# A retention and two mixture-of-experts layers on one core: decays taken relative to one fixed position, and the work of the attention put in order by tables

## The chip, the cores and the metric

One program runs on one core of a Trainium2 chip. The metric is the time of an execution on the device in microseconds (us). Five engines work side by side, each in its own fixed order: TensorE (PE in the profile; PEld is its loading of weights), VectorE (DVE), ScalarE (ACT), GpSimd (POOL) and SyncE (SP), which issues all the DMAs. An engine whose next instruction waits for a semaphore holds everything behind it.

## The reference, cut to what matters

Shapes: batch 2, 8 heads, 768 positions, head size 64. So there are 1536 tokens of width 512.

```
gamma = 1.0 - 2.0 ** (-5.0 - arange(H))
for t in range(S):                                   # the attention
    state = gamma * state + k[t] (outer) v[t]
    y[t]  = (1 / sqrt(D)) * q[t] @ state
x = y.reshape(B * S, H * D)
logits = x @ w_gate; P = exp(logits - max)           # first mixture, 8 experts
for _ in range(8): P /= P.sum(1); P /= P.sum(0); P *= N / E
out = sum over e of P[:, e] * (relu(x @ w1[e]) @ w2[e])
# second mixture, 4 experts: the same with p = domain_probs / its row sum
```

## The kernel before, in words

The attention is done in 12 chunks of 128 positions, 6 of each batch (chunk i, with c its place in the batch). For each chunk q, k (as head size by position) and kn, v (position by head size) are loaded, 256 KB each; the last chunk of a batch needs no kn. Heads go in pairs, so a [128, 512] tile holds all 8.

- Scores (`att_scores`, L242): 8 matmuls k by q into two PSUM banks. DVE multiplies both by a mask that holds the decay (L246), which gives `a`.
- `att_prep` on POOL: `ks` is kn scaled by a decay (L225), `qs` is q scaled by a decay and by the 1/sqrt(D) (L231).
- State (`att_decay`, `att_state`): POOL decays the state held in SBUF into `sg` (L253), PE makes the chunk's own part (L263), and DVE adds both into the other one of two tiles S (L276, two instructions; a copy at L271 for a batch's first chunk).
- Output (`att_out`): PE adds qs by S (L288) and v by a (L293) in one of two PSUM banks called chain. The chunks c = 0 to 2 go through `first_half`, the others through `second_half`. These make the inputs of the first layer's matrix products: every input is kept as a high part (fp32r, made by ACT) and a low part (the rest), and four differences (T1 to T4) are needed, since the products are done by a 7-product scheme. ACT copies the bank to SBUF (L144, L155), DVE makes the differences (L152) and the low parts (L78).

The attention is written out by hand as a loop over the chunks: load and prepare chunk i+2, scores of i+1, state of i, the leftover pieces of chunk i-1, output of i. Chunk buffers: three for q, k and v, two for kn. Into the same loop go the loads and splits of the first expert's weights (w1: four raw blocks of 256 KB; sums at L117, high parts on ACT at L124, low parts on POOL at L128) and the gate's logits (L347: 8 matmuls for the first half of a batch, 12 for the second).

Then come 48 units: each does one half of one expert for one batch, 168 matmuls of 128x384 (L494). Their order is set by tables: each piece has a place, and all pieces are sorted by it (`UNIT_AT`, `W_AT`). The first unit needs only batch 0's inputs and the first weights; its first product M1 is the first row of L494. Pieces of the last chunk are left for it.

Of the kernel before, what the change touches and what calls it, by code (L numbers as in the profile page):

```python
# [14 lines left out]
C_MASK, C_QT, C_ID, C_ONE, C_G, C_K, C_SEL, C_END = 0, 1024, 1536, 1664, 1792, 1796, 1804, 1812  # L15
# [8 lines left out]
def retention_moe_moe(ctx: ExitStack, tc: tile.TileContext, qT, kT, kN, vN, cst, wg, dprob, w1a, w2a, w1b, w2b, out):  # L24
# [114 lines left out]
    def first_half(key, b, j, pa, xa):  # L139


        hi, lo = (t[:, :, j * P:(j + 1) * P] for t in xt[key, b]["A"])
        n = 4 if key == 1 else 2
        return [lambda: nc.scalar.activation(out=xa[:, 0:n], in_=pa[:, 0:n], func=AF.Copy), lambda: split(hi, lo, pa)]  # L144

    def second_half(key, b, j, pb, xa, xb, b21):


        x = {k: [t[:, :, j * P:(j + 1) * P] for t in v] for k, v in xt[key, b].items()}

        def sub(to, a, b_):
            nc.vector.tensor_tensor(out=to, in0=a, in1=b_, op=ALU.subtract)  # L152

        def b12():
            nc.scalar.activation(out=xb[:, 0:2], in_=pb[:, 0:2], func=AF.Copy)  # L155

        def sums13():
            sub(xa[:, 0:2], pb[:, 0:2], xa[:, 0:2])
            sub(xb[:, 0:2], pb[:, 2:4], xb[:, 0:2])

        def sums24():
            sub(xb[:, 2:4], pb[:, 2:4], xa[:, 0:2])
            sub(xa[:, 2:4], b21, xb[:, 2:4])

        return [b12, lambda: split(*x["B22"], pb[:, 2:4]), sums13, sums24,
                lambda: split(*x["TA"], xa), lambda: split(*x["TB"], xb)]

    def x_block(key, b, k):
        kk, o = {"B11": ("A", 0), "B21": ("A", 2), "B22": ("B22", 0), "T1": ("TA", 0), "T2": ("TB", 2),
                 "T3": ("TB", 0), "T4": ("TA", 2)}[k]  # L170
        return [t[:, o:o + 2] for t in xt[key, b][kk]]

    with tc.manual_schedule():
# [40 lines left out]
        qtab = ap1.tile([P, NPR, CK], F32, name="qtab")
        nc.sync.dma_start(out=qtab, in_=cst[:, C_QT:C_ID].rearrange("p (h t) -> p h t", h=NPR))
        load_att(2, ("q", "k"))
        load_att(1, ("kn", "v"))
        nc.sync.dma_start(out=small[:, 0:C_G - C_ID], in_=cst[:, C_ID:C_G])

        def att_prep(i):  # L220
            b, c = chunks[i]
            t = att_in[i]
            if c < NCK - 1:
                ks = ap2.tile([P, H, D // H], F32, tag="ks", name="ks")
                nc.gpsimd.tensor_tensor(  # L225
                    out=ks, in0=t["kn"].rearrange("p (h d) -> p h d", h=H),
                    in1=ktab.unsqueeze(2).to_broadcast([P, H, D // H]), op=ALU.mult)
                t["ks"] = ks
            if c > 0:
                qs = ap2.tile([P, NPR, CK], F32, tag="qs", name="qs")  # L230
                nc.gpsimd.tensor_tensor(out=qs, in0=t["q"], in1=qtab, op=ALU.mult)  # L231
                t["qs"] = qs

        def att_scores(i):
            t = att_in[i]

            a = t["a"] = ap2.tile([P, 2, NPR, CK], F32, tag="a", name="a")
            p_ = [ps(), ps()]
            for pr in range(NPR):
                for z in range(2):  # L240
                    o = slice(64 * z, 64 * z + 64)
                    nc.tensor.matmul(  # L242
                        p_[z][:, pr * CK:(pr + 1) * CK], t["k"][o, pr, :], t["q"][o, pr, :],
                        start=True, stop=True, skip_group_check=True)
            for z in range(2):
                nc.vector.tensor_tensor(  # L246
                    out=a[:, z], in0=quads(p_[z]), in1=quads(mask[:, z]), op=ALU.mult)

        def att_decay(i):
            c = chunks[i][1]  # L250
            if 0 < c < NCK - 1:
                sg = att_in[i]["sg"] = ap1.tile([P, NPR, P], F32, tag="sg", name="sg")
                nc.gpsimd.tensor_tensor(out=sg, in0=S[c % 2], in1=gtab.unsqueeze(2).to_broadcast([P, NPR, P]), op=ALU.mult)  # L253

        def att_state(i):
            b, c = chunks[i]
            t = att_in[i]
            if c == NCK - 1:
                return
            p_ = ps()  # L260
            for h in range(H):
                o = slice(64 * (h % 2), 64 * (h % 2) + 64)
                nc.tensor.matmul(  # L263
                    p_[o, h * 64:(h + 1) * 64], t["ks"][:, h, :], t["v"][:, h * 64:(h + 1) * 64],
                    start=True, stop=True, skip_group_check=True)
            pv = p_.rearrange("p (r e) -> p r e", r=NPR)
            new = S[(c + 1) % 2]
            if c == 0:
                for z in range(2):
                    o = slice(64 * z, 64 * z + 64)  # L270
                    nc.vector.tensor_copy(new[o, :, o], pv[o, :, o])  # L271
            else:
                sg = t["sg"]
                for z in range(2):
                    o = slice(64 * z, 64 * z + 64)
# [667 lines left out]
```

## Time and profile before

| what | value |
|---|---|
| median of 3 runs | 1506.4 us (1506.12 to 1507.52) |
| profiled execution, span from first to last instruction | 1502.8 us |
| PE busy | 1474.6 us, 98% of the span |
| DVE, POOL, ACT busy | 73%, 69%, 49% |
| granted TensorE clock, mean | 0.993 of full speed |

The profile gives the span of its execution, which is 3.6 us under the median of the runs; what lies around the span is in that difference. A share of 98% for PE is an average over two stages: the attention at the start, in the first two of the 40 slices of the page, and the units. A busy PE counts matmuls as they lie in its pipeline, so where blocks are short, busy does not mean at its peak.

### The profile page before, as it was taken

To read this page: it belongs to the slowest core of one execution; us is meant where nothing else is said; L and a number is where in the kernel's file an instruction comes from. 1 tells how busy PE (TensorE), PEld (TensorE's weight loads), DVE (VectorE), ACT (ScalarE), POOL (GpSimd) and SP (SyncE) were. 2 spreads that over 40 slices of the span, in tenths; PEclk is the share of its full clock that TensorE was granted. 3 is DMA by queue.
4 is the path that set the end of the run, shared out by engine and by line. 5 is a ranking of instruction groups with operands and counts; after the bars stand their busy time and mean duration, and the time that the engine had idled before them with its cause. 6 is when DMAs were issued, how large, how long until landed. Compare 5 with 4: busy or idle time off the path is not lost.

```text
span 1502.8 us, 24372 instructions
## 1 busy us (share of the span) xinstructions
PE 1474.6 (98%) x8778; PEld 1457.2 (97%) x8778; DVE 1097.7 (73%) x2079; ACT 742.2 (49%) x1589; POOL 1038.6 (69%) x901
## 2 busy tenths in 40 slices
PE   8899999999999999999999999999999999999998
PEld 6799999999999999999999999998999999999998
DVE  5868877677777767776776776788667767777776
ACT  2355454455455444545544544555655445545552
POOL 5756587686676766856865866769958668677682
PEclk9999999999999999999999999999999999999999
DMA  9310112211211211121122112111121121121112
GB/s 294 113 29 29 30 50 61 67 39 40 78 39 39 58 59 39 39 78 40 39 57 61 39 39 78 40 39 39 57 60 39 40 77 39 39 73 45 39 47 88
DMA packets 97432, 86.23 MB, mean 57 GB/s; under 512 B 9376, under 2 KB 85280, under 8 KB 97312
## 3 DMA queue, kind: packets, MB, share of 16 engines
q1 hardware_dynamic: 97312, 84.69, 18.5%
q8 instruction: 68, 1.11, 0.3%
q14 instruction: 52, 0.43, 0.1%
HBM read 81.45 MB, written 3.22 MB: 56 GB/s over the span
## 4 chain that ended last, share of the span: by engine, by line
PE 88%; POOL 4%; DVE 4%; issue 2%; DMA 1%; SPq 0%; ACT 0%; DVEq 0%; POOLq 0%
PE ps L494 49%; PE chain L494 37%; POOL w L128 1%; POOL raw L117 1%; POOL h L554 1%; DMA kn<-in_kN 1%; DVE acc L481 1%; PE ps L347 1%; DVE xl L78 0%; DVE ps L481 0%; DMA raw<-in_w2a 0%; POOL acc L543 0%; POOL ev L617 0%; DMA k<-in_kT 0%; DVE acc L152 0%
## 5 line engine op out<-in xcount | busy, mean ns | idle before, releaser
L494 PE MATMUL ps<-h,w 128*128 128x384 f32 x2304 | 432.3, 335 | 1.8 <-POOL h L554 1.6
L494 PE MATMUL ps<-xh,w 128*128 128x384 f32 x1536 | 431.4, 336 | 0.6 <-ACT ev L478 0.5
L494 PEld LDWEIGHTS ps<-h,w 128*128 128x128 f32 x2304 | 402.2, 188 | 4.1 <-POOL h L554 3.1
L128 POOL TENSOR_TENSOR w<-raw,w 128x512 fp32r<-128x512 f32 x266 | 356.8, 1345 | 55.9 <-ACT w L124 55.8
L494 PE MATMUL chain<-xh,w 128*128 128x384 f32 x1152 | 332.9, 336 | 3.2 <-ACT ev L478 2.3
L494 PE MATMUL chain<-h,w 128*128 128x384 f32 x1728 | 333.2, 335 | 2.5 <-DVE acc L481 1.8
L554 POOL TENSOR_TENSOR h<-ev,h 128x384 fp32r<-128x384 f32 x288 | 292.9, 1032 | 45.0 <-ACT h L478 43.8
L617 POOL TENSOR_TENSOR ev<-ev,fac 128x384 f32<-128x384 f32 x96 | 98.3, 1024 | 301.9 <-DVE ps L613 301.2
L494 PEld LDWEIGHTS chain<-h,w 128*128 128x128 f32 x1728 | 302.5, 188 | 3.9 <-DVE acc L481 1.8
L494 PEld LDWEIGHTS ps<-xh,w 128*128 128x128 f32 x1536 | 282.8, 189 | 1.2 <-ACT ev L478 1.2
L124 ACT ACTIVATE w<-raw 128x512 fp32r<-128x512 f32 x336 | 205.1, 624 | 151.7 <-POOL raw L117 130.0
L117 POOL TENSOR_TENSOR raw<-raw 128x512 f32<-128x512 f32 x188 | 244.5, 1301 | 20.0 <-POOL w L128 13.7
L494 PE MATMUL ps<-xl,w 128*128 128x384 f32 x768 | 257.9, 336 | 0.0
L481 DVE TENSOR_TENSOR acc<-chain,acc 128x384 f32<-128x384 f32 x272 | 150.5, 554 | 105.3 <-PE chain L494 104.2
L554 DVE TENSOR_TENSOR h<-ps,h 128x384 fp32r<-128x384 f32 x384 | 210.8, 550 | 11.8 <-ACT h L478 3.3
L478 ACT ACTIVATE h<-ps 128x384 fp32r<-128x384 f32 x384 | 186.4, 488 | 65.5 <-DVE ps L481 61.8
L494 PEld LDWEIGHTS chain<-xh,w 128*128 128x128 f32 x1152 | 211.9, 188 | 4.8 <-ACT ev L478 3.1
L494 PE MATMUL chain<-xl,w 128*128 128x384 f32 x576 | 193.1, 335 | 1.8 <-POOL xl L758 1.8
L478 ACT ACTIVATE chain<-ps 128x384 f32<-128x384 f32 x192 | 92.0, 479 | 204.2 <-DVE acc L481 171.1
L481 DVE TENSOR_TENSOR acc<-ps,acc 128x384 f32<-128x384 f32 x272 | 145.3, 548 | 45.9 <-PE ps L494 45.9
L478 ACT ACTIVATE h<-ev 128x384 fp32r<-128x384 f32 x288 | 149.6, 520 | 45.1 <-DVE ev L557 40.9
L494 PEld LDWEIGHTS ps<-xl,w 128*128 128x128 f32 x768 | 145.3, 189 | 0.0
(116 smaller groups left out, 1181.6 us busy)
## 6 DMA issues: line engine op xcount, KB each, us to landing
fac<-rows SPq DMA_DIRECT2D x46, 384.0 KB
raw<-in_w1a SPq DMA_DIRECT2D x128, 128.0 KB
raw<-in_w2a SPq DMA_DIRECT2D x64, 256.0 KB
raw<-in_w1b SPq DMA_DIRECT2D x64, 128.0 KB
raw<-in_w2b SPq DMA_DIRECT2D x32, 256.0 KB
q<-in_qT SPq DMA_DIRECT2D x12, 256.0 KB
k<-in_kT SPq DMA_DIRECT2D x12, 256.0 KB
v<-in_vN SPq DMA_DIRECT2D x12, 256.0 KB
```

The lines of the kernel that those rows point to most:

```text
L117: eng.tensor_tensor(out=raws[s, k], in0=raws[s, a], in1=raws[s, b], op=op)
L124: nc.scalar.activation(out=t[0], in_=raws[s, k], func=AF.Copy)
L128: eng.tensor_tensor(out=lo, in0=raws[s, k], in1=f32(hi), op=ALU.subtract)
L347: nc.tensor.matmul(p_[:, 0:TH], l, r, start=(n == 0), stop=(n == len(mm) - 1))
L478: copy, relu = (lambda o, i, f=f: nc.scalar.activation(out=o, in_=i, func=f) for f in (AF.Copy, AF.Relu))
L481: nc.vector.tensor_tensor(out=out, in0=in0, in1=in1, op=op)
L494: nc.tensor.matmul(p_, l, r, start=(first and n == 0), stop=(n == len(mm) - 1), skip_group_check=True)
L554: eng.tensor_tensor(out=lo, in0=src, in1=f32(hi), op=ALU.subtract)
L617: nc.gpsimd.tensor_tensor(out=a22, in0=a22, in1=self.g_[:, 1], op=ALU.mult)
```

## The change

The decay of a key is now taken relative to one fixed position of the batch (the start of chunk `MID` = 2). v is scaled once per chunk by gamma to a power that depends on its position (`vs`, POOL), and this vs serves both the state and the product with a. The mask is then only 0 or 1, one [128, 128] tile. The state needs no decay between chunks: PE sums it over all chunks of a batch in one PSUM bank, which stays taken (`state`), and ACT copies it to S. q is used as it is. The output of a chunk is multiplied by a table (`scale`, DVE); the tables of chunks 1 to 5 are made by ACT, four instructions each, out of the one before (`dt`).

The differences are made in another form: the output no longer is copied by ACT; in chunks c = 0 to 2 scale writes it to SBUF, in the others it stays in its bank, and T2 and T3 go to a third bank (`self.q`). Low parts of A and TA go to POOL save for four pieces named in `ON_VECTOR`; three of the four weight sums go there as well. The second half's logits take 8 matmuls, with weights that hold the needed sums. At the start PE clears 9 times a bank with zeros in place of two fp32 matmuls; two matmuls before the units (L842) go.

Buffers for q, k, v and kn are four each. The constants shrink (the mask from 512 KB to 64 KB). The order of all pieces of the attention comes from tables by chunk (`CHUNK_AT`, one number for each batch) and for the other pieces (`MISC_AT`); the first unit and the first weights have tables of their own (`UNIT0_AT`, `W0_AT`).

```diff
+    def low(t, src, eng):
+        eng.tensor_tensor(out=t[1], in0=src, in1=f32(t[0]), op=ALU.subtract)
+
+    def high(t, src):
+        nc.scalar.activation(out=t[0], in_=src, func=AF.Copy)
+
+    def sub(to, a, b_):
+        nc.vector.tensor_tensor(out=to, in0=a, in1=b_, op=ALU.subtract)
...
+                t[nm] = ap2.tile([P, NPR, CK] if nm in "qk" else [P, D], F32, tag=nm, name=nm, bufs=4)
...
+        def clear(bank):
+            nc.tensor.matmul(bank, zero[:, 0:P], zero, start=True, stop=True, skip_group_check=True)
...
+        state = ps()
+        for c_ in 4 * chain + [state]:
+            clear(c_)
+
+        mask = ap1.tile([P, CK], F32, name="mask")
+        nc.sync.dma_start(out=mask, in_=cst[:, C_MASK:C_V])
+        tabs = ap1.tile([P, C_DT - C_V], F32, name="tabs")
+        nc.sync.dma_start(out=tabs, in_=cst[:, C_V:C_DT])
+        vtab = tabs[:, 0:C_G - C_V].rearrange("p (c h) -> p c h", h=H)
...
+            def vs(self):
+                t = self.t
+                t["vs"] = ap2.tile([P, H, D // H], F32, tag="vs", name="vs")
                 nc.gpsimd.tensor_tensor(
+                    out=t["vs"], in0=t["v"].rearrange("p (h d) -> p h d", h=H),
+                    in1=vtab[:, self.c].unsqueeze(2).to_broadcast([P, H, D // H]), op=ALU.mult)
+
+            def dt(self):
+                c = self.c
+                if self.b == 0 and c > 0:
+                    dtab[c] = ap1.tile([P, NPR, CK], F32, name=f"dtab{c}")
+                    for r in range(NPR):
+                        nc.scalar.activation(out=dtab[c][:, r], in_=dtab[c - 1][:, r], func=AF.Copy, scale=gtab[:, r:r + 1])
...
+                nc.vector.tensor_tensor(
+                    out=t["a"][:, z], in0=quads(t["p"][z]), in1=mask.unsqueeze(1).to_broadcast([P, NPR, CK]), op=ALU.mult)
...
-            new = S[(c + 1) % 2]
-            if c == 0:
-                for z in range(2):
-                    o = slice(64 * z, 64 * z + 64)
-                    nc.vector.tensor_copy(new[o, :, o], pv[o, :, o])
-            else:
-                sg = t["sg"]
-                for z in range(2):
-                    o = slice(64 * z, 64 * z + 64)
-                    nc.vector.tensor_tensor(out=new[o, :, o], in0=pv[o, :, o], in1=sg[o, :, o], op=ALU.add)
...
+                        state[o, h * 64:(h + 1) * 64], t["kn"][:, h * 64:(h + 1) * 64], t["vs"][:, h, :],
+                        start=False, stop=True, skip_group_check=True)
+
+            def S(self):
+                if self.c < NCK - 1:
+                    nc.scalar.activation(out=S[(self.c + 1) % 2], in_=quads(state), func=AF.Copy)
...
+                            self.o[:, pr], S[c % 2][:, pr, :], t["q"][:, pr, :], start=(pr == 0), stop=False, skip_group_check=True)
...
+            def scale(self):
+                xs[self.i] = quads(spare(self.i % 5))
+                to = self.o if self.half else xs[self.i]
+                nc.vector.tensor_tensor(out=to, in0=self.o, in1=dtab[self.c], op=ALU.mult)
+
+            def hA(self):
+                high(self.x("A"), xs[self.i])
+
+            def lA(self):
+                low(self.x("A"), xs[self.i], lower(f"lA{self.i}"))
+
+            def t12(self):
+                self.xa, self.xt = xs[self.i - TPH], xs[self.i]
+                self.q = self.o if self.last else quads(ps())
+                sub(self.xt[:, 0:2], self.o[:, 0:2], self.xa[:, 0:2])
+                sub(self.q[:, 0:2], self.o[:, 2:4], self.xt[:, 0:2])
+
+            def t4(self):
+                sub(self.xt[:, 2:4], self.xa[:, 2:4], self.q[:, 0:2])
+
+            def t3(self):
+                sub(self.q[:, 2:4], self.q[:, 0:2], self.xa[:, 0:2])
...
+            def lTA(self):
+                low(self.x("TA"), self.xt, lower(f"lTA{self.i}"))
+
+            def hTB(self):
+                high(self.x("TB"), self.q)
+
+            def lTB(self):
+                low(self.x("TB"), self.q, nc.vector)
...
-            parts = [("B11", 0), ("B21", 2)] if half == 0 else [("B11", 0), ("T1", 0), ("B22", 2)]
-            mm = [(wgs[:, o + c, :], x[:, c, :]) for k, o in parts for c in range(2) for x in x_block(1, b, k)]
+            parts = [("B11", 0), ("B21", 2)] if half == 0 else [("B22", 4), ("T3", 6)]
...
+        CHUNK_AT = {'load': (-5.779, -1.553), 'vs': (-1.56, -1.499), 'dt': (-2.533, -3.312), 'scores': (-0.823, -0.993), 'state': (0.146, 0.42), 'S': (0.148, 0.44), 'm0': (-0.505, -0.474), 'm1': (-0.113, -0.254), 'scale': (0.925, 0.587), 'hA': (1.552, 0.777), 'lA': (1.716, 2.293), 't12': (1.096, 0.873), 'hB': (1.104, 1.418), 't4': (1.241, 1.22), 't3': (1.37, 0.999), 'lB': (1.579, 1.813), 'hTB': (1.765, 1.569), 'hTA': (1.354, 1.651), 'lTB': (2.108, 1.884), 'lTA': (1.935, 1.869), 'inter': (0.866, 0.251), 'av': (0.867, 0.252)}
+        ON_VECTOR = ('+S2', 'lA0', 'lA6', 'lTA11')
...
+        for _, _, f, a in sorted(todo, key=lambda e: e[:2]):
+            f(a)
...
-        for c_ in (chain[1], chain[0]):
-            x_ = xt[1, 0]["A"][0].rearrange("p c t -> p (c t)")[:, 0:512]
-            nc.tensor.matmul(c_, w1t[0, "A11"][0][:, 0, 0, :], x_, start=True, stop=True, skip_group_check=True)
...
+            for name, places in {**UNIT_AT, **(UNIT0_AT if k == 0 else {})}.items():
```

On SP the four blocks of w1 are now loaded in three places: A11 ahead of chunk 3, A22 ahead of chunk 6 (with the gate's small inputs behind it), A21 and A12 between chunks 6 and 7. Before, all four stood behind chunk 5's v. Nothing else stands ahead of chunk 11's loads.

The order on two engines. PE from the scores of chunk 11 on, before (q, k are a chunk's inputs, a its masked scores, S the state's tiles, acc the gate's weights in L347):

```order
L242 MATMUL ps<-q,k 128x128 x8
L263 MATMUL ps<-v,ks 64x64 x8
L288 MATMUL chain<-qs,S_86 128x128 x4
L293 MATMUL chain<-a,v 64x128 x8
L288 MATMUL ps<-qs,S_87 128x128 x4
L293 MATMUL ps<-a,v 64x128 x8
L842 MATMUL chain<-xh,w_547 128x512 x2
L347 MATMUL ps<-xh,acc 128x384
```

The same from chunk 11's scores on, after:

```order
L260 MATMUL ps<-q,k 128x128 x8
L299 MATMUL chain<-q,S_86 128x128 x4
L306 MATMUL chain<-a,vs 64x128 x8
L285 MATMUL ps<-vs,kn 64x64 x8
L395 MATMUL ps<-xh,acc 128x384
L395 MATMUL ps<-xl,acc 128x384
```

Here 16 rows of L395, the logits of batch 0, now stand between the state of chunk 10 and the last two rows of the attention, L299 and L306 of chunk 11. After these come the 8 logits of batch 1's first half and M1, as before. In the kernel before, batch 0's logits stood ahead of chunk 10's and of chunk 11's scores.

DVE in the stretch from chunk 7's to chunk 8's scores, before (xl are low parts, raw the weight sums, S the state):

```order
L246 TENSOR_TENSOR a<-ps,mask 128x512 x2
L276 TENSOR_TENSOR S_86<-ps,sg 64x4x64 x2
L78 TENSOR_TENSOR xl<-chain,xh 128x4x128
L78 TENSOR_TENSOR xl<-acc,xh 128x4x128 x2
L117 TENSOR_TENSOR raw<-raw 128x512
L246 TENSOR_TENSOR a<-ps,mask 128x512 x2
```

And after, from chunk 7's masks on (dtab is the table of `scale`):

```order
L268 TENSOR_TENSOR a<-ps,mask 128x512
L313 TENSOR_TENSOR acc<-chain,dtab_119 128x512
L268 TENSOR_TENSOR a<-ps,mask 128x512
L141 TENSOR_TENSOR xl<-ps,xh 128x4x128
L268 TENSOR_TENSOR a<-ps,mask 128x512
L313 TENSOR_TENSOR acc<-chain,dtab_184 128x512
```

The state's two rows are gone, scale has come in between the two masks of a chunk, and the low parts that stand there read a PSUM bank.

## Rows read from the trace of the kernel before

**Rows 1.** Windows: span, busy us and count of each engine, clock, DMA share, GB/s.

```profile
0.00:10.00 10.00, 6.77 (x38) 4.04 (x40) 1.95 (x4) 1.28 (x1) 2.23 (x7) 1.00 0.81 279
10.00:20.00 10.00, 8.96 (x123) 7.92 (x124) 4.70 (x9) 2.17 (x4) 7.66 (x7) 0.83 0.94 286
20.00:30.00 10.00, 9.47 (x135) 8.11 (x134) 7.59 (x17) 2.06 (x6) 7.17 (x9) 1.00 0.96 288
30.00:40.00 10.00, 7.70 (x120) 6.69 (x120) 9.63 (x27) 3.70 (x9) 3.85 (x4) 1.00 0.98 331
40.00:50.00 10.00, 3.86 (x56) 3.34 (x56) 9.89 (x13) 3.16 (x6) 10.00 (x8) 0.89 0.62 207
50.00:60.00 10.00, 9.90 (x90) 8.64 (x91) 8.99 (x12) 3.04 (x6) 8.35 (x7) 0.77 0.08 30
...
300.00:1503.00 1203.00, 1194.58 (x6861) 1190.85 (x6859) 876.25 (x1626) 608.15 (x1305) 843.61 (x728) 1.00 0.17 51
```

**Rows 2.** Timeline (start, us, then the instructions), PE at the end of the attention.

```profile
68.91 0.34 PE L347 MATMUL ps<-xh,acc 128*128 128x384 f32 x1
...
70.32 0.33 PE L494 MATMUL ps<-xh,w 128*128 128x384 f32 x1
```

**Rows 3.** Waits of PE before 70.3 us: total, times, longest.

```profile
PE chain L288 <- DVE xl L78: 6.9, 3, 5.7
PE ps L242 <- DMA k<-in_kT: 2.4, 2, 1.9
```

**Rows 4.** Waits of SP's DMA queue before 75 us: total, times, longest.

```profile
SPq L190 <- PE chain L293: 14.5, 5, 8.2
```

**Rows 5.** Timeline, PE, first scores of batch 1.

```profile
31.57 1.16 PE L242 MATMUL ps<-q,k 64*128 64x128 f32 x16 [1.94 <-DMA k<-in_kT]
```

**Rows 6.** Timeline, PE, one chunk of batch 0 in order.

```profile
22.82 0.69 PE L263 MATMUL ps<-v,ks 128*64 128x64 f32 x16
...
23.44 1.15 PE L288 MATMUL chain<-qs,S 128*128 128x128 f32 x8
...
24.52 1.09 PE L293 MATMUL chain<-a,v 128*64 128x128 f32 x16
...
25.55 1.16 PE L242 MATMUL ps<-q,k 64*128 64x128 f32 x16
```

**Rows 7.** Timeline, PE after its longest wait.

```profile
50.10 2.05 PE L288 MATMUL chain<-qs,S 128*128 128x128 f32 x8 [5.67 <-DVE xl L78]
```

**Rows 8.** Groups by line and shape, DVE, before 70.3 us: busy, mean ns, idle before.

```profile
L246 DVE TENSOR_TENSOR a<-ps,mask 128x512 f32<-128x512 f32 x24 | 15.3, 681 | 12.5 <-PE ps L242 12.4
L78 DVE TENSOR_TENSOR xl<-acc,xh 128x512 fp32r<-128x512 f32 x8 | 10.1, 1296 | 0.0
L276 DVE TENSOR_TENSOR S<-ps,sg 64x256 f32<-64x256 f32 x16 | 6.7, 419 | 5.8 <-POOL sg L253 5.7
...
L117 DVE TENSOR_TENSOR raw<-raw 128x512 f32<-128x512 f32 x4 | 5.1, 1286 | 0.0
L78 DVE TENSOR_TENSOR xl<-chain,xh 128x512 fp32r<-128x512 f32 x6 | 4.2, 692 | 0.2
```

**Rows 9.** Groups by line and shape, POOL, before 70.3 us.

```profile
L231 POOL TENSOR_TENSOR qs<-q,qtab 128x512 f32<-128x512 f32 x10 | 13.8, 1384 | 0.0
L225 POOL TENSOR_TENSOR ks<-kn,small 128x512 f32<-128x512 f32 x10 | 11.5, 1154 | 18.6 <-DMA kn<-in_kN 18.6
L128 POOL TENSOR_TENSOR w<-raw,w 128x512 fp32r<-128x512 f32 x7 | 10.1, 1454 | 6.2 <-ACT w L124 6.2
L253 POOL TENSOR_TENSOR sg<-S,small 128x512 f32<-128x512 f32 x8 | 9.2, 1152 | 0.0
```

**Rows 10.** Groups by line and shape, ACT, before 70.3 us.

```profile
L144 ACT ACTIVATE acc<-chain 128x512 f32<-128x512 f32 x6 | 3.6, 593 | 27.3 <-PE chain L293 21.7 <-DVE xl L78 5.5
...
L155 ACT ACTIVATE acc<-chain 128x256 f32<-128x256 f32 x5 | 1.9, 379 | 12.0 <-PE chain L293 7.9 <-PE ps L242 4.1
```

**Rows 11.** Timeline, DVE, lows read from SBUF, POOL idle and POOL busy.

```profile
35.73 1.29 DVE L78 TENSOR_TENSOR xl<-acc,xh 128x512 fp32r<-128x512 f32 x2
...
40.94 3.43 DVE L78 TENSOR_TENSOR xl<-acc,xh 128x512 fp32r<-128x512 f32 x2
```

More of the change, by code (lines that the diff above doesn't have):

```diff
@@ L214, in retention_moe_moe @@
[L214 to L224, printed above, removed]
-                nc.gpsimd.tensor_tensor(
[L226 to L232, printed above, removed]
@@ new lines, in retention_moe_moe @@
+        ON_VECTOR = ('+S2', 'lA0', 'lA6', 'lTA11')
+        FIRST_AT = {'scores': -3.475, 'm1': -0.632, 'm0': -1.999, 'vs': -2.199, 'state': -0.219, 'scale': 1.183}
+        LAST_AT = {'t12': -2.17, 'hB': 1.35, 't4': -2.164, 'lB': 3.021, 't3': 3.1, 'hTB': 3.2, 'hTA': -0.104, 'lTB': 3.3, 'lTA': 0.876}
+        MISC_AT = {'loadA21': 4.489, 'loadA11': -3.686, 'loadA22': 2.159, 'loadA12': 5.383, 'small': 2.226, 'wgb': 7.217, 'wgs': 7.56, 'dp': 8.875, 'rows': 9.541, 'w2': 11.969, 'logits0': 10.877, 'logits1': 11.07, 'A11': 4.834, '+S3': 5.416, 'A22': 3.433, '+S1': 6.405, '+S2': 7.911, 'A12': 8.552, '+S4': 11.449, 'S1': 8.942, 'S2': 9.009, 'S3': 9.846, 'S4': 11.978}
@@ new lines, in misc @@
+        def misc(k):
+            if k.startswith("load"):
+                load_w1(0, (k[4:],))
+            elif k[0] == "+":
+                sum_of(0, k[1:], lower(k))
+            elif k[0] in "AS":
+                split_hi(0, k)
+                split_lo(0, k, lower(k))
+            else:
+                {"small": get_small, "wgb": sum_wg, "wgs": prep_wg, "dp": prep_dp, "rows": lambda: keep_rows(2, small_in["dpt"]),
+                 "w2": lambda: load_w2(0), "logits0": lambda: logits(0, 0), "logits1": lambda: logits(0, 1)}[k]()
@@ new lines, in retention_moe_moe @@
+        todo = [(p, n, misc, k) for n, (k, p) in enumerate(MISC_AT.items())]
+        final = []
+        for i in range(len(chunks)):
+            ch = Chunk(i)
+            for name, places in CHUNK_AT.items():
+                pos = places[ch.b]
+                if name in (LIGHT if ch.half else HEAVY) or (name == "load" and i < 3):
+                    continue
+                f = getattr(ch, name)
+                if ch.last and name in LAST_AT:
+                    final.append((LAST_AT[name], f))
+                    continue
+                if i == 0:
+                    pos = FIRST_AT.get(name, pos)
+                todo.append((i + pos, len(todo), lambda g: g(), f))
@@ L853, in retention_moe_moe @@
         for k, un in enumerate(units):
-            for name, places in UNIT_AT.items():
+            for name, places in {**UNIT_AT, **(UNIT0_AT if k == 0 else {})}.items():
                 for i, pos in enumerate(places):
@@ L873, in retention_moe_moe @@
                         at(k * L + pos, to_x2, un.b, name, c)
-        for pos, f in zip((-1, -0.5, 0, 0.5, 15.8, 17.0, 18.5, 20.3), todo + late):
+        for pos, f in final:
             at(pos, f)
```

270 lines of the change are left out of this document (118 added, 152 removed).

## The prediction

> **What bounds the kernel now.** I read the busy times by stretch first, then the end of the attention in the timeline, then the waits of PE and of SP, then the groups of instructions by shape.
>
> From 300 us on PE is busy 1194.6 of 1203 us at full clock [rows 1]: the units are bound by PE, and 9 us are all that any edit outside the attention could win there. M1, the first product of the first unit, starts at 70.32 us [rows 2]. So the question is when M1 starts after the change. What comes behind it is the same 168 matmuls for each of 48 units.
>
> The attention has two halves of different kinds. Up to 40 us the DMAs bound it: they are busy 0.81 to 0.98 and move 279, 286, 288 and 331 GB/s, 11.84 MB in all [rows 1], and PE waits for k of chunk 6 until 31.57 us [rows 5]. From 40 us on the DMA rate falls to 207 while DVE is busy 9.89 and POOL 10.00 of 10 us and PE 3.86 [rows 1]. The longest wait of PE is 5.7 us for a DVE low part [rows 3], and SP waits 14.5 us for PE to give back chunk buffers [rows 4]. So the second half is bound by DVE and POOL, which hold PE, which holds the loads. When PE comes back at 50.10 us it does so at the lower clock: eight instructions of L288 take 2.05 us [rows 7] against 1.15 [rows 6].
>
> **The change part by part.** DVE: the state's 16 instructions of 0.419 us (6.7 us) go, with a wait of 5.7 us for POOL's decay behind which the rest of DVE's queue stood [rows 8]. New are 12 scales of 128x512 from PSUM; the nearest row is the mask's 0.681, so 8.2 us. Moved to POOL are three of four sums (3.9 us), four lows of A (2.8) and five of TA (6.5); the lows of TB now read PSUM and fall from the 1.296 to the 0.692 row, 6 x 0.60 = 3.6 [rows 8]. In all DVE has 15 us less. The lows from SBUF are the slow ones where POOL works beside them: a pair took 1.29 us with POOL idle and 3.43 with POOL busy [rows 11]; after the change two are left in the stretch.
>
> What DVE still has to do from chunk 7's scores to chunk 11's scale is 8 masks, 4 scales (12 x 0.68), one sum and one low (2.6), about 1 us of gate inputs and for chunks 9 and 10 six pieces each at 0.42 (by L276, equally wide) and one low at 0.69: 18 us in a stretch that comes out at 25 below. It is no longer the bound.
>
> POOL: qs (13.8 us) and sg (9.2) go; vs comes 12 times where ks came 10 (+2.3); 12 lows and sums come, at L128's 1.454, 17.4 [rows 9]. So 3.3 us less, in a shorter attention: it is nearly as full, and a rival below rests on it.
>
> ACT: 10 copies of the state at 0.593 and 20 pieces of the tables come. For one piece of 128x128 there is no row; above, it is the 0.379 of a piece twice as wide, below, a quarter of the 0.593 row, 0.15 [rows 10]. I take 0.26, by a line through 512 and 256 wide; 5.2 us. 12 copies go (6 x 0.593 and 6 x 0.379, 5.8 us). ACT gains 5 us of work and stays under half busy; the tables hide under the DMA-bound first half (at 0.15 or 0.379, 2 us either way, they still do).
>
> SP: the loads no longer wait for PE, since a fourth buffer lets the load of chunk 11 go once chunk 7 is done. Up to and with k of chunk 11 the queue holds 45 tiles of 262 KB (11.80 MB), w1 (1.05), the table (0.26) and 0.27 of small things: 13.38 MB. 11.84 are moved in the first 40 us, the rest takes 1.54 / 0.331 = 4.7 us to 1.54 / 0.288 = 5.3. So at about 45 us it has moved, if the first 40 us keep their rates. For chunk 7's k the same sum is 9.18 MB: 8.53 in 30 us, and 2.0 us more, 32.0. How long after its bytes a tile is there I read from chunk 6's k before: 8.57 MB were queued up to it, 9.05 had moved when PE went on at 31.57, so 1.5 us late. Thus scores of chunk 7 can start between 32.0 and 33.5; I take 33.0, and 46.5 for k of chunk 11.
>
> PE: one chunk takes 0.62 (state), 1.08 (q by S), 1.03 (v by a) and 1.1 (scores, 1.16 with its drain) [rows 6], 3.8 us with nothing waited for. With the small gaps at each hand-over I take 4.2; the bounds are 3.8 and 4.9, where the last adds a wait for one scale and one narrow piece of DVE, 0.68 and 0.42 [rows 8]. From chunk 7's scores on: scores and v by a of chunks 7 and 6, a clear and state 6 (2.9 us; chunk 6 has no q by S), then three whole chunks to chunk 11's scores: 33.0 + 2.9 + 12.6 = 48.5, behind the 46.5 at which its k is there. Then 4.2 for scores 11, chunk 10's output and state; 16 logits at 0.176 (eight take 70.32 - 68.91 [rows 2]), 2.8; q by S and v by a of chunk 11, 2.1; 8 logits, 1.4. M1 starts at 59.0 and no longer at 70.32: 11.3 us earlier. The state's copy by ACT between state 10 and chunk 11's q by S lies under the 16 logits; without these it would cost 0.6.
>
> In the first unit the other half's logits are 8 and not 12: 4 x 0.176 = 0.7. The two matmuls of L842 lie before 68.91 and are in the 11.3 already. The nine clears take the place of two fp32 matmuls while the first tiles are on the way: nothing, and 1 us if the tiles were earlier. The first unit's new tables I take at nothing: its products are the same, M6 still waits for one ACT copy; the bounds are 1.5 us won and 2 lost, from the 9 us that PE idles in all of the rest.
>
> Sum: the span of 1502.8 less 12.0 is 1490.8. The runs' median is 3.6 us over this execution's span; that lies outside the change, so 1494.4. With 32.0 and 3.8 for a chunk M1 starts at 56.4 and the time is 1491.8; with 33.5 and 4.9 at 62.3, 1497.7.
>
> **A rule that speaks against it.** In rows 1 the clock is 0.83 in the second 10 us, 1.00 in the next two, where PE waits for chunks of data, and 0.89 where PE is busy 3.86 of 10 us. After that idle stretch a block costs twice as much [rows 7]. The Trainium skill (TensorE: Matmul & The Clock Gate, HAM oscillation) has it that a kernel whose short blocks of matmuls wait for DMAs can fall back to the lower clock before each block. The trace agrees for the stretch without work, and not for 20 to 40 us, where blocks of 4 us waited for DMAs at full clock. By that rule the stretch that I put at full clock would run at half.
>
> **The rivals.**
>
> The POOL tail. With v of chunk 10 there at 43.8 (by the sum above), POOL does two vs, four pieces and a small one (2.3 + 5.8 + 0.2) to 52.1, four more (5.8) to 57.9; behind the last, a sum, stands an ACT high part (0.6), and behind that on ACT the copy that M6 waits for, due at 60.0. The margin is 1.5 us. If POOL's pieces took half as long again (7.0 us more), that copy would come at 65.5 and PE would wait 5.5 us: 1499.9. For it: POOL was busy 10.00 of 10 us between 40 and 50 [rows 1]. Against: L128's mean already holds that stretch.
>
> PE earlier. If the DMAs run at 331 GB/s throughout, chunk 7's k is there at 9.18 / 0.331 + 1.5 = 29.2, and with 3.8 a chunk M1 starts at 53.6: 1489.0. For it: 331 is the rate of the last window before the buffers ran out. Against: the windows ahead of it have 286 and 288 at a share of 0.94 to 0.96.
>
> The clock. At half clock a chunk costs 6.9, as 1.08 becomes 2.0 [rows 7]; for chunks 7 to 10, 4 x 3.1 = 12.4 us, which eats the gain: 1506.8.
>
> Slower: the banks. The state keeps one of six PSUM banks; a chunk's scores take two, and in the second half of a batch its differences a third. If the scores of the next chunk then wait for the low part of TB, a chunk is serial: 1.1 scores, 1.4 masks, 2.1 on PE, 0.7 scale, 1.7 differences, 0.6 high, 0.7 low, 8.3 us against 4.2. For all six such chunks that is 24.6 us, 1519. It decides from the third serial chunk on (12.0 / 4.1 = 2.9). Against it: the places of the scores lie before those of the differences, so that a bank is free when masks are done.
>
> **How the numbers follow.** The forecast has 0.70, the POOL tail 0.14, PE earlier 0.09, the clock 0.04, the banks 0.03. What a measurement of this kernel can tell from no change is 0.2%, 3 us: the first three are faster (0.93; with a part of the clock case 0.94), the clock case holds the same, the banks slower. The range takes in the forecast's own, and the tail and PE earlier up to their times: 1489 to 1500.5.
>
> **What would show it.** M1 starts between 57 and 62 us; SP does not wait for PE's output matmuls; scores of chunk 7 start within 32 to 34 and wait for k; DVE's busy share from 40 to 50 us is clearly under 9.9 of 10; PE's clock stays 1.00 from 20 us on. The units behind take as long as before, within 2 us. It is wrong if PE still waits for DVE or POOL for several us in one place, or if the gain at M1 is lost in the first two units.

## The result, and the profile after

| what | before | after |
|---|---|---|
| median of the runs, us | 1506.26 (4 runs, 1505.20 to 1507.52) | 1491.06 (4 runs, 1489.83 to 1493.10) |
| ratio, 95% interval | | 0.9898, 0.9884 to 0.9912 |
| profiled execution, span | 1502.8 us | 1488.1 us |
| M1, first product of the first unit | 70.32 us [rows 2] | 57.81 us |
| from M1 to the end of the span | 1432.5 us | 1430.3 us |

The change makes the kernel 15.2 us, 1.0%, faster. The forecast was 1494.4, its range 1489.0 to 1500.5. Of the 14.7 us that the span loses, 12.5 are gone at M1 and 2.2 behind it.

Windows of after, to be laid beside [rows 1]: span, busy us and count of PE, PEld, DVE, ACT and POOL, then clock, DMA share, GB/s.

```profile
10.00:20.00 10.00, 9.38 (x124) 8.69 (x125) 4.91 (x8) 7.68 (x24) 3.46 (x5) 0.83 1.02 350
20.00:30.00 10.00, 10.00 (x151) 9.06 (x149) 7.37 (x14) 5.00 (x11) 6.21 (x6) 1.00 0.82 236
30.00:40.00 10.00, 8.71 (x123) 7.43 (x121) 9.68 (x21) 4.23 (x8) 9.92 (x9) 1.00 1.06 377
40.00:50.00 10.00, 10.00 (x155) 9.07 (x152) 8.41 (x17) 5.54 (x13) 8.29 (x11) 1.00 0.48 170
...
300.00:1488.00 1188.00, 1179.37 (x6780) 1174.75 (x6778) 865.54 (x1603) 598.14 (x1283) 832.25 (x718) 1.00 0.17 51
```

From 40 to 50 us PE is busy 10.00 of 10 us where it was 3.86; DVE falls from 9.89 to 8.41. The units behind are as before: PE idles 8.4 us of the long last window before and 8.6 after.

The timeline of PE from chunk 7 on, after: start, us, then the instructions.

```profile
33.57 1.16 PE L260 MATMUL ps<-q,k 64*128 64x128 f32 x16 [1.29 <-DMA k<-in_kT]
...
36.73 1.16 PE L260 MATMUL ps<-q,k 64*128 64x128 f32 x16
37.82 1.16 PE L299 MATMUL chain<-q,S 128*128 128x128 f32 x8
38.91 1.09 PE L306 MATMUL chain<-a,vs 128*64 128x128 f32 x16
39.84 0.64 PE L285 MATMUL ps<-vs,kn 128*64 128x64 f32 x16
40.40 1.16 PE L260 MATMUL ps<-q,k 64*128 64x128 f32 x16
...
47.74 1.16 PE L260 MATMUL ps<-q,k 64*128 64x128 f32 x16
...
54.31 1.05 PE L299 MATMUL ps<-q,S 128*128 128x128 f32 x8
...
57.81 0.34 PE L548 MATMUL ps<-xh,w 128*128 128x384 f32 x1
...
59.61 0.44 PE L548 MATMUL chain<-xh,w 128*128 128x384 f32 x1 [0.56 <-ACT chain L532]
```

Behind one wait of 1.29 us for k of chunk 7, PE waits for nothing until M6. A chunk takes 40.40 - 36.73 = 3.67 us, its four blocks back to back, and chunk 11's scores stand at 47.74, three chunks behind chunk 8's.

Waits of PE up to M1, after (total, times, longest), which answer to [rows 3]:

```profile
PE ps L260 <- DMA k<-in_kT: 3.0, 2, 1.7
...
PE ps L285 <- POOL vs L243: 0.7, 1, 0.7
```

Of SP's queue, for [rows 4]:

```profile
SPq L171 <- PE chain L299: 0.9, 2, 0.5
```

No wait of PE for DVE is left. The queue's wait for PE to give back chunk buffers has fallen from 14.5 us to 0.9 in the rows shown, and from 15.2 to 1.8 over all rows with PE as releaser.

The groups by line and shape up to 57.8 us, after, which answer to [rows 8 to 10]: busy, mean ns, idle before.

```profile
L268 DVE TENSOR_TENSOR a<-ps,mask 128x512 f32<-128x512 f32 x24 | 16.0, 682 | 13.4 <-PE ps L260 13.4
L313 DVE TENSOR_TENSOR acc<-chain,dtab 128x512 f32<-128x512 f32 x6 | 4.1, 688 | 1.7 <-PE chain L306 1.7
...
L243 POOL TENSOR_TENSOR vs<-v,tabs 128x512 f32<-128x512 f32 x12 | 12.5, 1044 | 18.9 <-DMA v<-in_vN 13.0 <-PE chain L306 4.8 <-PE ps L285 1.0
L141 POOL TENSOR_TENSOR xl<-acc,xh 128x512 fp32r<-128x512 f32 x9 | 11.5, 1284 | 0.0
...
L252 ACT ACTIVATE dtab<-dtab,tabs 128x128 f32<-128x128 f32 x20 | 6.2, 388 | 4.4 <-DMA dtab<-in_cst 4.4
```

Up to M1 DVE is busy 38.0 us for 51.0 before, POOL 37.5 for 45.1, ACT 28.3 for 19.8.

### The profile page after: what moved, and what is told of

Read it like the earlier page. It is cut to its first block, busy times and chain, and to the rows that moved or that the text cites. A ratio compares the mean times of both kernels' runs of the same rounds, so it can differ in the third digit from the quotient of the medians.

```text
span 1488.1 us, 24327 instructions
## 1 busy us (share of the span) xinstructions
PE 1466.2 (99%) x8774; PEld 1450.4 (97%) x8774; DVE 1081.2 (73%) x2056; ACT 749.1 (50%) x1610; POOL 1031.6 (69%) x900
## 4 chain that ended last, share of the span: by engine, by line
PE 90%; POOL 4%; DVE 2%; issue 2%; DMA 1%; SPq 0%; ACT 0%; DVEq 0%; POOLq 0%; ACTq 0%
PE ps L548 50%; PE chain L548 37%; POOL w L129 1%; POOL raw L118 1%; POOL h L608 1%; PE ps L260 1%; DMA k<-in_kT 1%; PE chain L306 1%; DVE acc L535 1%; PE chain L299 1%; POOL xl L812 0%; PE ps L395 0%; DMA raw<-in_w2a 0%; POOL ev L671 0%; DVE ps L535 0%
## 5 line engine op out<-in xcount | busy, mean ns | idle before, releaser
L118 POOL TENSOR_TENSOR raw<-raw 128x512 f32<-128x512 f32 x191 | 248.7, 1302 | 20.2 <-POOL w L129 13.7
```

What stands on the lines that cost most here:

```text
L118: eng.tensor_tensor(out=raws[s, k], in0=raws[s, a], in1=raws[s, b], op=op)
```

## The experiments

Ratios are to executions of the kernel before taken beside each run. M1, span and chunk 7 are read from the one profiled execution; "chunk 7" is the start of its scores and, in brackets, the wait for k ahead of it.

| run | median, us (runs) | ratio, interval | chunk 7 | M1 | span |
|---|---|---|---|---|---|
| after | 1491.06 (4) | 0.9898, 0.9884 to 0.9912 | 33.57 [1.29] | 57.81 | 1488.1 |
| e5_after_again | 1492.74 (5) | 0.9899, 0.9883 to 0.9916 | 32.42 [1.88] | 58.16 | 1490.8 |
| e1_loop_order | 1496.52 (4) | 0.9926, 0.9906 to 0.9945 | 33.87 [0] | 60.00 | 1497.5 |
| e2_before_buf4 | 1504.90 (10) | 0.9982, 0.9973 to 0.9992 | | 70.42 | 1500.9 |
| e3_after_buf3 | 1497.42 (4) | 0.9934, 0.9917 to 0.9950 | 34.48 [2.45] | 61.90 | 1494.6 |
| e4_state_copy_on_dve | 1493.84 (4) | 0.9908, 0.9891 to 0.9925 | 32.70 [2.36] | 60.62 | 1491.5 |
| e11_lows_on_dve | 1497.91 (5) | 0.9939, 0.9926 to 0.9951 | 32.77 [0.21] | 62.75 | 1495.8 |
| e6_logits12 | 1495.78 (5) | 0.9923, 0.9910 to 0.9936 | 33.29 [1.98] | 58.25 | 1492.6 |
| e7_old_unit_tables | 1490.96 (4) | 0.9893, 0.9877 to 0.9909 | 33.26 [2.29] | 57.53 | 1487.3 |
| e8_small_loads_late | 1492.79 (5) | 0.9907, 0.9892 to 0.9922 | 32.14 [0] | 59.68 | 1492.7 |
| e9_dpr_last | 1490.61 (4) | 0.9891, 0.9875 to 0.9907 | 31.48 [1.06] | 55.76 | 1488.4 |
| e10_dpr_last_table_later | 1493.22 (5) | 0.9913, 0.9897 to 0.9928 | 34.68 [0] | 60.03 | 1494.3 |

The theory: the gain is that of the attention, made by work taken off DVE and by loads that go without waiting for PE, so that M1 comes earlier. The rivals: that one part alone (order, buffers, unit tables, logits) holds it, or that another engine stands just behind DVE.

**e5_after_again: the change once more, as a control.** A blank line added at the end of the file.

> The changed kernel once more, beside the next three on one chip. M1 at 57 to 59 us, chunk 7's scores at 33 to 34 behind a wait for k of about 1 us; the time is 1490 to 1493.

M1 came at 58.16 and the ratio is the same (0.9899 for 0.9898). Chunk 7 was there 1.15 us earlier than in the first profile, and PE lost it again: behind the wait the clock fell. PE of this run:

```profile
32.42 1.16 PE L260 MATMUL ps<-q,k 64*128 64x128 f32 x16 [1.88 <-DMA k<-in_kT]
33.51 1.86 PE L306 MATMUL chain<-a,vs 128*64 128x128 f32 x16
35.30 0.80 PE L181 MATMUL ps<-zero 128*128 128x512 f32 x1
36.03 1.12 PE L285 MATMUL ps<-vs,kn 128*64 128x64 f32 x16
37.08 1.16 PE L260 MATMUL ps<-q,k 64*128 64x128 f32 x16
```

From scores to scores that is 4.66 us, where the first profile has 3.16: 1.5 us for one fall (the granted clock is 0.50 from 34 to 37 us, 1.00 up to 33). So one execution of the same kernel can lose 1.5 us ahead of M1 that another keeps, and single profiles are read with that in mind below.

**e1_loop_order: the change's work in the order of the loop before.**

```diff
-        CHUNK_AT = {'load': (-5.779, -1.553), 'vs': (-1.56, -1.499), ..., 'scores': (-0.823, -0.993), ...
+        CHUNK_AT = {'load': (-2.0, -2.0), 'vs': (-1.99, -1.99), ..., 'scores': (-0.9, -0.9), ...
```

> The changed kernel's work in the loop order of the kernel before (load and scale chunk i+2, scores and masks of i+1, state of i, leftover pieces of i-1, output of i), through other numbers in the table by chunk; the other tables stay. Theory (less work on DVE and POOL is what lets PE go on): M1 starts at 60 to 66 us instead of 57.8, some waits of PE come back, the time is 1493 to 1499. Rival (the order of the pieces does it): M1 starts at 68 to 72 us and the time is 1502 to 1507.

M1 at 60.00: ten of the 12.5 us come without the new order of the chunks' pieces; the tables for the other pieces stayed. The tail that I gave as a rival is there: M6 now waits. PE of this run, then its ACT:

```profile
63.47 0.44 PE L548 MATMUL chain<-xh,w 128*128 128x384 f32 x1 [2.24 <-ACT chain L532]
```

```profile
60.34 0.63 ACT L125 ACTIVATE w<-raw 128x512 fp32r<-128x512 f32 x1 [1.90 <-POOL raw L118]
60.87 0.61 ACT L144 ACTIVATE xh<-acc 128x512 fp32r<-128x512 f32 x1
...
62.94 0.47 ACT L532 ACTIVATE chain<-ps 128x384 f32<-128x384 f32 x1 [0.61 <-DVE chain L897]
```

ACT stands 1.90 us for POOL's last sum, then works off what queued behind, then waits 0.61 us for a DVE clear before the copy that M6 needs. So the order is worth 2.2 us at M1 and 1.7 at M6 (2.24 against 0.56), 3.9 of the 5.5 us between the medians (4.2 by the two ratios). What is left is of the size of one fall of the clock, and behind the wait at M6 the clock did fall in this execution (0.64 from 64 to 66 us and 0.51 from 66 to 68).

**e2_before_buf4 and e3_after_buf3: the buffers alone, and all but the buffers.** In before all four inputs of a chunk get four buffers; in after q, k, v get three and kn two, as before had.

```diff
-    ..., F32, tag=nm, name=nm, bufs=2 if nm == "kn" else 3)
+    ..., F32, tag=nm, name=nm, bufs=4)
```

> The kernel before with four buffers each for q, k, v and kn. Theory (DVE and POOL hold PE): SP's wait of 14.5 us goes, M1 stays within 1 us of 70.3, the time is 1505 to 1507. Rival (late loads held PE): M1 starts at 64 us or earlier, the time is 1500 or less.

> The changed kernel with three buffers for q, k, v and two for kn, as before. Theory: chunk 11's k is held until chunk 8's state and scores are done at about 44 us and is there at 47 to 48, just when its scores are due (47.7): M1 at 57.8 to 59.3, the time 1490.5 to 1493. Rival (the buffers carry the gain): M1 at 62 us or later, 1495 or more.

In before the buffers do nothing for M1 (70.42 for 70.32). PE's waits there, up to 62 us, are again for DVE, as in [rows 3]:

```profile
PE chain L288 <- DVE xl L78: 4.8, 3, 2.1
PE chain L288 <- DVE acc L152: 4.6, 1, 4.6
```

SP's wait for PE's output matmuls does not go, as I had expected, but falls from 14.5 to 5.1 us. The median of that run is 2.4 us lower, 0.18%, with M1 where it was in its profile; why was not followed further, and the profile has two falls of the clock fewer behind M1 than before's.

In after, taking the buffers away costs 4.1 us at M1 and 5 to 6 in the time (5.4 by the two ratios, 6.4 by the medians), against the 0 to 1.5 that I expected at M1: a miss, with the time where the rival put it (1495 or more) and M1 0.1 us short of the rival's 62. But 8.4 of the 12.5 us at M1 stay without the buffers. Waits of PE, then of SP, in e3:

```profile
PE ps L260 <- DMA k<-in_kT: 7.3, 6, 2.4
```

```profile
SPq L171 <- PE ps L285: 11.0, 5, 4.6
```

The loads wait for PE again (11.0 us), and from chunk 9 on the scores wait for each k (1.10, 0.87, 0.99 us), so that a chunk takes 4.6 to 4.9 us and not 3.67. The releaser is the state's product (L285), which gives back kn: the two buffers of kn hold the queue, and q and k of the next chunk stand behind. I had looked at chunk 11's k alone; the queue stands already from 33.1 to 37.7 us, for a kn. The two parts are worth more together than apart, 4.1 us at M1 for nothing alone. The reading that fits the waits is that with DVE slow a fourth buffer holds data that PE can't take yet, and with PE fast kn's two are too few.

**e4_state_copy_on_dve and e11_lows_on_dve: how much room DVE has.** In e4 DVE copies the state to S in place of ACT; in e11 all sums and all low parts of A and TA are on DVE. Of the four pieces that `ON_VECTOR` names in after, three are low parts and one is a sum.

```diff
-                    nc.scalar.activation(out=S[(self.c + 1) % 2], in_=quads(state), func=AF.Copy)
+                    nc.vector.tensor_copy(S[(self.c + 1) % 2], quads(state))
```

```diff
-        ON_VECTOR = ('+S2', 'lA0', 'lA6', 'lTA11')
+        ON_VECTOR = ('+S1', '+S2', '+S3', '+S4', 'lA0', 'lA1', 'lA2', 'lA6', 'lA7', 'lA8', 'lTA3', 'lTA4', 'lTA5', 'lTA9', 'lTA10', 'lTA11')
```

> The changed kernel with the ten copies of the state to SBUF on DVE instead of ACT, 10 x 0.69 us more there. Theory (DVE is no longer the bound, busy 38 of 57.8 us): M1 at most 1 us later, the time 1491 to 1493. Rival (DVE is still what sets the pace in the second half of a batch): 4 to 7 us later, 1495 to 1498.

> The changed kernel with all sums and all low parts of A and TA on DVE: 12 pieces of 128x512 more there, 0.68 us each where POOL is idle and up to 1.3 beside it, 8 to 15 us. Theory (DVE has no more than some 5 us to spare in the stretch from 30 to 57 us, by the run with the state's copies on DVE): PE waits for DVE again, M1 at 62 to 68 us, the time 1495 to 1501. Rival (the state's work alone was the bound): M1 under 60 us, 1493 or less.

e4 misses my bound of 1 us: M1 is 2.8 us later than in after. Chunk 7 starts 0.9 us earlier; a fall of the clock behind the wait of 2.36 us takes 1.5, as in e5; the four chunks behind take 4.1 to 4.5 us each, 2.2 more in all. The first of them waits 0.63 for a DVE low part; in the others v by a is held in its middle for the second mask, which on DVE now stands behind the state's copy, the first mask and the scale (chunk 8's second mask runs from 43.73 to 44.41 us, its v by a starts at 44.00). So for these chunks DVE sets the pace again, as the rival had it, for 2.2 us where the rival had 4 to 7. In the time e4 is not told apart from after: 0.9908 for 0.9898, with intervals that overlap. e11 came within its range, 4.9 us late at M1. Its windows, then its waits of PE up to M1:

```profile
30.00:40.00 10.00, 6.96 (x79) 5.39 (x81) 9.93 (x20) 2.92 (x7) 3.06 (x4) 1.00 1.00 366
40.00:50.00 10.00, 8.79 (x130) 8.01 (x129) 9.79 (x20) 5.31 (x12) 4.41 (x7) 1.00 0.43 134
```

```profile
PE chain L299 <- DVE xl L141: 2.4, 2, 1.2
...
PE ps L260 <- DVE xl L141: 1.1, 1, 1.1
PE chain L306 <- DVE xl L141: 1.1, 1, 1.1
```

DVE is full again (9.93, 9.79) and PE waits 4.6 us for its low parts. So the prediction was right that DVE is no longer the bound in after, but it is near: what was moved to POOL decides some 5 us. The same shows in e8 and e10, where chunk 7's scores need not wait for k: there chunk 7's q by S waits 0.53 us for a DVE low part.

**e6_logits12 and e7_old_unit_tables: the small terms.** e6 gives the second half's logits the three parts and 12 matmuls of before. e7 sorts the first unit and the first weights by the general tables.

```diff
-            parts = [...] if half == 0 else [("B22", 4), ("T3", 6)]
+            parts = [...] if half == 0 else [("B11", 0), ("T1", 0), ("B22", 2)]
```

```diff
-            for name, places in {**UNIT_AT, **(UNIT0_AT if k == 0 else {})}.items():
+            for name, places in UNIT_AT.items():
...
-                for name, pos in (W_AT if un.s else W0_AT).items():
+                for name, pos in (W_AT if un.s else {n: p for n, p in W_AT.items() if n.lstrip('+hl')[0] in 'BT'}).items():
```

> The changed kernel with the 12 matmuls of before for the logits of a batch's second half. Theory: 4 x 0.173 us more on PE ahead of M1 (which then starts 0.7 us later) and as much in the first unit: 1.4 us over the changed kernel of the same call. Rival (these matmuls lie in gaps of PE): no change, under 0.5 us.

> The changed kernel with the tables of the other units for the first unit and the first weights too. My term for these tables was nothing, with bounds of 1.5 us won and 2 lost: M1 as in the changed kernel, the time within 1 us. Rival (the tables carry the 2.2 us that the span won behind M1): 1.5 to 3 us slower, with the new waits of PE between 58 and 140 us.

e6 has M1 where e5 has it (58.25 for 58.16), but only since e5 lost 1.5 us to the fall at chunk 7. From chunk 11's scores to M1, where nothing waits in either, e6 takes 10.80 us and e5 10.07, so the four matmuls cost 0.73 there, as costed. Chunk 11's scores in e6, then in e5:

```profile
47.45 1.16 PE L260 MATMUL ps<-q,k 64*128 64x128 f32 x16
```

```profile
48.09 1.16 PE L260 MATMUL ps<-q,k 64*128 64x128 f32 x16
```

The median is 3.0 us longer than e5's, taken beside it, and all five times of e6 (1494.64 to 1496.94) lie above all five of e5 (1489.87 to 1493.51). So the sign is right. Both halves of the 1.4 that I costed are there: in the first unit the other half's 12 matmuls take 2.10 us (84.22 to 86.32), where e5's 8 take 1.40 (84.12 to 85.52). The further 1.6 us of the median are not explained. e7 shows no difference in time from e5 or after: the new unit tables are worth nothing that can be measured, as costed. The traces do show that they cost one wait, 10.2 us behind M1 in after (0.85 us; e5, e6 and e9 have it too), at a place where neither before nor e7 waits:

```profile
68.05 0.45 PE L548 MATMUL chain<-xh,w 128*128 128x384 f32 x1 [0.85 <-ACT chain L532]
```

**e8, e9 and e10: the small loads in SP's queue.** After's SP has one odd row. Its timeline around the gate's small inputs:

```profile
19.90 0.37 SPq L201 DMA_DIRECT2D wgr<-in_wg  x1
20.57 0.37 SPq L203 DMA_DIRECT2D dpr<-in_dprob  x1
21.24 2.63 SPq L411 DMA_DIRECT2D small<-in_cst  x1
23.97 1.08 SPq L171 DMA_DIRECT2D q<-in_qT  x1
```

An issue that mostly takes 0.3 to 0.5 us takes 2.63 here, behind the load of the domain probabilities (dpr), which comes in pieces of 4 numbers. The DMA rate of that window is 236 GB/s, between 350 and 377, and k of chunk 7 stands behind it. e8 moves all three small loads behind chunk 9's inputs and the work on them with it; e9 moves dpr alone behind chunk 11's; e10 is e9 with the load of the output's table behind chunk 1's v and kn.

```diff
-        MISC_AT = {..., 'small': 2.226, 'wgb': 7.217, 'wgs': 7.56, 'dp': 8.875, 'rows': 9.541, ...}
+        MISC_AT = {..., 'small': 7.46, 'wgb': 8.3, 'wgs': 8.56, 'dp': 8.875, 'rows': 9.541, ...}
```

```diff
-            nc.sync.dma_start(out=dpr, in_=dprob.rearrange("(t p) e -> p t e", p=P))
...
+        MISC_AT = {..., 'small': 2.226, 'dpr': 9.46, ..., 'dp': 10.8, 'rows': 10.85, ...}
```

> The changed kernel with the loads of the gate's inputs and of the small constants behind chunk 9's loads instead of ahead of chunk 6's (and the two pieces that use them first moved from 7.2 and 7.6 to 8.3 and 8.6). Theory (chunk 7's k is the gate of the whole stretch, and these loads, during which SP stood from 21 to 25 us, delay it): chunk 7's scores start at 32 us with no wait for k, M1 at 55.5 to 56.7, the time 1.2 to 2.5 us under the changed kernel's. Rival (w1 and the chunks' own bytes set k's landing, or another chunk's wait takes its place): M1 within 0.5 us of 57.8.

> The changed kernel with one load moved: domain_probs (24 KB in pieces of 16 bytes), from ahead of chunk 6's loads to behind chunk 11's, and its two uses to 10.8. Theory (this load holds SP for 2.6 us at the next issue, and so chunk 7's k, the gate of the stretch, without another chunk being hit this time): chunk 7's scores start at 30 to 32.5 us with no wait over 0.3 us, M1 at 55.5 to 56.8, the time 1 to 2.5 us under the changed kernel's 0.990 of before, so a ratio of 0.988 to 0.9895. Rival (another load or piece takes the wait's place): M1 at 57.5 to 60.

> As the run before, and the table's load behind chunk 1's v and kn instead of ahead of them. Theory (with the gate at chunk 7 gone, PE is bound from its first chunks on, and their kn 0.8 us earlier counts): M1 0.5 to 0.9 us under the run before. Rival (ACT makes the tables later, and the state's copy stands behind two of them): M1 0 to 1 us over it.

e8 only moves the trouble. Chunk 7 no longer waits, but the queue stands later, ahead of chunk 10's loads:

```profile
34.14 0.45 SPq L203 DMA_DIRECT2D dpr<-in_dprob  x1
34.78 4.69 SPq L411 DMA_DIRECT2D small<-in_cst  x1
```

Its PE then waits 0.69 us for k of chunk 10 and 1.36 for a state copy on ACT, and M1 is at 59.68, later than my theory and its rival had it. In e9, with nothing behind it to hold, chunk 7 starts 2.1 us earlier than in after, though it still waits 1.06 us for its k, where I had expected 0.3 at most, and M1 comes at 55.76, the earliest of all runs:

```profile
20.45 0.34 SPq L410 DMA_DIRECT2D small<-in_cst  x1
21.18 0.34 SPq L171 DMA_DIRECT2D q<-in_qT  x1
```

That confirms the load as the cause of the stand. In the time it hardly shows: 1490.61, an interval that covers after's, since the span from M1 on came out 2.3 us longer than after's, with falls of the clock around 90 and 1017 us. e5 has falls at the same two places, and against it e9's span is 2.4 us shorter, all of it ahead of M1. No version is shown to beat the changed kernel.

e10 shows what the tables on ACT cost when their cover goes. Its ACT, then its PE:

```profile
10.78 2.44 ACT L251 ACTIVATE dtab<-dtab,tabs 128x128 f32<-128x128 f32 x8 [3.31 <-DMA dtab<-in_cst]
13.13 0.57 ACT L290 ACTIVATE S<-ps 128x512 f32<-128x512 f32 x1
```

```profile
13.81 1.12 PE L284 MATMUL ps<-vs,kn 128*64 128x64 f32 x16 [2.75 <-issue]
14.86 2.08 PE L259 MATMUL ps<-q,k 64*128 64x128 f32 x16
```

Eight pieces of the table, late by their load, hold the first state copy, PE stands 2.75 us, and the clock is at its lower level until 20 us (granted mean 0.66 from 10 to 20 us). Chunk 7 comes at 34.68 without a wait for its k, and M1 at 60.03, 4.3 us over e9's. The rival was right that the state's copy would stand behind the tables, but had put it at 1 us at most. In e9 the same place costs 1.45 us.

## Why the prediction was right, step by step

**M1 bounds it, and comes 11.3 us earlier.** Right; 12.5. Sum and measurement go side by side from the profile: chunk 7 at 33.57 for 33.0 (+0.6); chunks 7, 6 and a state in 3.16 for 2.9 (+0.3); four chunks of 3.67 for 4.2 (-2.1); the rest as costed. The step that was mis-sized is the chunk: I added small gaps at each hand-over to 3.8, and there are none. From start to start v by a takes 0.93 where [rows 6] have 1.03, and the state 0.56 for 0.62: v by a is now followed by the state and the state by scores, and the distance depends on what comes next (ahead of scores v by a takes 1.03 in after too, in chunk 5). 3.67 lies under my lower bound.

**DVE is no longer the bound.** Right, with 13.0 us less work for the 15 that I worked out, and less room than the text gave: e4 and e11 show it. No run keeps the state's decay on POOL and DVE in the changed kernel, so what the fixed position is worth by itself is not shown. Taken away singly, the moves of low parts and sums, the buffers and the order cost 4.9, 4.1 and 2.2 us at M1; these need not add.

**POOL.** Busy 7.6 us less for the 3.3 forecast. Pieces took 1.28 and 1.29 where [rows 9] has 1.454, and vs 1.044 for 1.154. The trace of before holds a likely cause: there the same piece ks takes 1.04 us while DVE's pieces read PSUM, and 1.49 beside two of DVE's sums, which have both inputs in SBUF (44.30 to 47.27 us):

```profile
39.70 1.04 POOL L225 TENSOR_TENSOR ks<-kn,small 128x512 f32<-128x512 f32 x1 [0.54 <-DMA kn<-in_kN]
...
45.23 1.49 POOL L225 TENSOR_TENSOR ks<-kn,small 128x512 f32<-128x512 f32 x1
```

In after fewer such pieces are left on DVE. No run changes this alone. The rival of the tail did not come about in after (M6 waits 0.56 us, and the ACT copy waits for PE, not for POOL), and did in e1: the margin is real, and with the old order it is gone.

**ACT's tables.** Mis-sized: 0.388 a piece, above my upper bound of 0.379, where I took 0.26 by a line through 512 and 256 wide (which gives 0.27). Those rows have a constant scale, these pieces one that is read from a tile, and lie 0.12 over the line. The Trainium skill (ScalarE: Activation LUTs, What ACT_TABLE_LOAD costs) states a fixed part of 186 ns, 0.833 ns for each column and about 93 ns for each operand given by pointer; an estimate from these is 186 + 93 + 128 x 0.833 = 386 ns. The trace agrees, at 388. Back to back they overlap, so that 20 took 6.2 us and not 7.8. The cost was hidden in after, and is 1.4 to 2.8 us of PE's wait in e3, e7, e9, e10 and e11, ahead of a wait for k that swallows it in all but e10.

**SP and the DMAs.** Chunk 7 was expected from 32.0 to 33.5: 33.57 in the first profile, 32.42 in the second, with 1.3 to 2.5 us of waiting in six of the runs. That the sum by bytes met it is in part luck: errors cancel. The first three windows moved 242, 350 and 236 GB/s, 8.28 MB, where I had carried over 8.53 from before; the rest came at 377, above the 331 that I took as the upper end. In the third window lies the stand of 2.6 us behind dpr that I did not see; without it, in e9, the three move 9.40 MB. It could have been read in the trace of before, on the load that is issued behind dpr:

```profile
14.68 2.18 SPq L190 DMA_DIRECT2D q<-in_qT  x1
```

k of chunk 11 was no limit; nothing waited for it.

**The clock.** 1.00 from 20 us on, as forecast, in the first profile; in e5 and e4 it fell behind waits for chunk 7's k of 1.88 and 2.36 us, and in e6, e7 and e3 it did not behind 1.98, 2.29 and 2.45. The rule that I weighed (the Trainium skill, TensorE: Matmul & The Clock Gate, HAM oscillation) is thus at work in some executions, once and not at each chunk, at 1.5 us and not 12.4.

**Behind M1.** -2.2 us for the -0.7 of the logits, just over the 2 us that I allowed. From 60 us on the profile of before has four windows of 10 us with a clock of 0.83 to 0.91, from three falls, after's none; e5, of the same kernel, has two falls and takes 1432.6 us from M1 on. e2, whose units are those of before, has one fall and takes 1430.5, after's 1430.3 within 0.2. So most of the 2.2 us is luck of the clock, and the logits' 0.7 (2.10 for 1.40 us on PE in e6 and e5) is lost in it.

**Around the span.** The 3.6 us carried over was no constant: it is 1.7 us in the profiled execution after, and 1.7 to 3.2 in all runs listed. The median of before had been set against a span at the lower end of its own (1502.2 to 1507.6). Of the 4.6 us by which the profiled execution of after lies under the forecast, 1.9 are this, 1.5 what lies behind M1 and 1.2 M1 itself.

## What to carry to other kernels

Read where the bound engine gives back its time, and count what stands next in line for it: here work given back to DVE, the old buffers and the old order, which brought POOL's tail out, each cost 2 to 5 us at M1, and a part that was worth nothing there alone (four buffers) was worth 4 us with the others. A chunk that nothing holds cost the distance from block start to block start in a stretch without waits (3.67 us), not the sum of its blocks plus an allowance (4.2). Before a queue's time is summed by bytes, look for issues that take several times the usual, and for what the row ahead of them loads.

## What the runs showed of the hardware

- A load in pieces of 4 numbers holds the issue behind it on its queue: that takes 2.18 us in before, 2.63 in after and 4.69 in e8, where most others take 0.3 to 0.5. In e9, with that load at the queue's end, the stand is gone.
- The clock falls in some executions of the same kernel and not in others. In the first profile of after it fell behind a wait of 1.72 us at 10.62 (granted clock 0.50 from 11 to 14 us, 1.00 from 15 on); in e5 it did not fall there, behind 0.92 at 8.90, but at chunk 7. A fall costs about 1.5 us, and profiles whose M1 differs by less than that can't be ranked by it.
- The places recur. Of the 13 profiles 9 fall 31 to 35 us behind M1, though PE has no wait there, at or behind 24 small matmuls of 8 columns (2.84 us in e5); after, e2, e4 and e7 do not. And 8 fall 957 to 963 us behind M1, in e5 behind a wait of 1.79 us; e6 has the same wait and no fall.
- POOL and DVE slow each other where both work from SBUF: a pair of DVE's low parts takes 3.43 us beside POOL and 1.29 without [rows 11], and POOL's ks 1.49 beside such DVE pieces and 1.04 without.
- An ACT piece of 128 columns with its scale in a tile takes as long as one of 256 columns with a constant scale: 388 and 379 ns.
